# Chunked attention and a gated feed-forward layer: the first round of products in two token halves, and other places for one unit's load, two units' steps and a scaling

## The chip, the cores and the metric

One core of one Trainium2 chip runs the whole kernel. The metric is the device time of one execution in microseconds; 0.1% of it is 0.9 us.

## What is computed

Attention over chunks of 64 tokens (8 sequences, 8 heads, 576 tokens, head size 64), then root-mean-square normalization and a gated feed-forward layer on 4608 tokens with a model width of 512 and an inner width of 1536, all in float32:

```python
scores = scale * q_c @ k_c.T                    # per chunk of 64 tokens and head
attn = exp(scores - max(scores)); attn /= sum(attn) + 1e-9
x = (attn @ v_c) as (4608, 512)
xn = x / sqrt(mean(x * x) + 1e-6) * rms_g
g = xn @ w_gate
out = (g * sigmoid(g) * (xn @ w_val)) @ w_out
```

## The kernel before

**Products.** A float32 operand is split into a high and a low part that TensorE multiplies at its faster float32 rate; a product of two split operands is three matmuls, high by high, high by low and low by high. Tokens go in blocks of 512 (t = 0 to 8). A block's tokens, transposed, stand in four pairs of tiles, `xh[dt]` and `xl[dt]` (dt = 0 to 3, 128 of the 512 model columns each). The inner width goes in 12 slices of 128 (f = 0 to 11); for each, 12 matmuls of 128x512 make `ps_g` and 12 make `ps_v`. ScalarE takes the silu of `ps_g` (`sg`, line 583 or 619), VectorE multiplies it by `ps_v`. The banks of `ps_g` (and in block 0 of `ps_v`) come from a pool of two.

**Units.** Attention goes in units of 256 tokens, two to a block. Units 0 and 1 stand ahead of all products. Their tokens are transposed and split by `x_transpose_unit` (line 546): transposes into one bank for two dts, then for each dt `x_split`, a scaled copy on ScalarE (the high part, line 523) and a subtraction on VectorE (the low part, line 524).

**Block 0 (t = 0).** Units 2 and 3 are computed between its products. The weights come as 64-bit numbers and are converted on the fly, `conv_start`, `conv_join` and `conv_end` (lines 183 to 220), mostly on VectorE. `gated(f, ...)` (line 574) calls `up` twice, then silu, product and split into `gh` and `gl`; `down` (line 624) multiplies the result of the slice before with `w_out`. A unit's tokens are normalized by `norm_unit` (line 490); its inner function `scale` (line 512), called at f = 4 and 9, multiplies them by `ri_u`, which GpSimd makes (line 510). From f = 9 on, `out_sides` (line 649) makes sums of `w_out` on VectorE (lines 659, 667, 672) for later blocks. At f = 11, `x_transpose` (line 536) brings the tokens of units 2 and 3 into `xh` and `xl`. In this part the framework's planner orders each engine's instructions, by program order, by what is ready in its own model of time, and with the instructions under `urgent()` ahead.

**Blocks 1 and 2.** Here each engine's order is the program's own. `gated_pair` (line 595) makes a slice's 24 products, and after each group of 12 one step of a hand-written list runs, 48 steps in all (step 0 to 23 in block 1, 24 to 47 in block 2; where a slice is taken by dt, its two steps stand at its end). The list `at` is filled in the loop over `UNIT_AT` (line 41), then with `sides` and `out_sides`. For each of the units 4 to 9, `UNIT_AT` has the steps of its 11 parts in `unit_steps` (line 1030 on): load of q and k (one buffer for all units), scores and exponentials (`first`), load of the values (a buffer shared with the tokens, two in all), sums and turn (`second`), away to DRAM, back as `eT` (`third`, line 377, one buffer), products with the values and norm (`fourth`, lines 392, 406, 462), scaling (line 417), turn (line 423), away (line 428), back into `x` (line 435). Within a step the units come in order of their number, then the sums of the weights. All these DMAs stand on SP's one queue in program order. At f = 11 of block 1 the tokens of units 4 and 5 replace those in `xh` and `xl` dt by dt (the turn-over); units 6 and 7 come into `x` after that. GpSimd makes the sums of the other weights (`sides`, line 690), in steps `SIDE_AT`, and the small steps of a norm.

The later blocks take two token blocks at a time by another scheme and are not touched.

## Time and profile before

| what | us |
|---|---|
| median of 3 runs | 904.32 (903.79 to 904.64) |
| the profiled execution | 903.54 |
| its span in the profile | 901.8 |
| TensorE busy | 875.2 (97%) |
| VectorE busy | 672.1 (75%) |
| ScalarE busy | 438.1 (49%) |
| GpSimd busy | 171.6 (19%) |

The profile is one execution, 0.78 us under the median; 1.7 us of it lie outside the span. Times in rows are from the span's start. TensorE's column PE is matmuls, PEld its weight loads, which go on beside them; the ends of matmuls are modelled, so a row's duration is longer than the distance to the next one's start, and it is the distance that counts. A row with an idle time in brackets tells what ended the engine's wait. A share of busy time over the whole span says little: the 75% of VectorE is far more in the first block and less later.

### The profile page before, as it was taken

Reading aid. Unit: us, or ns where it says so; the run is one execution under the profiler, and the core shown is the slowest. Engines: PE = TensorE matmul, PEld = TensorE weight load, DVE = VectorE, ACT = ScalarE, POOL = GpSimd, SP = SyncE. Lnnn points to the kernel's source line nnn. Section 1 sums busy time; section 2 is a strip of 40 time slices with the busy share of each in tenths; the row PEclk is TensorE's granted clock in tenths of the full one; section 3 lists DMA queues with packets and bytes.
Section 4 is the critical chain, followed back from the end, with each engine's and each line's share of the span. In section 5 each row is a group of like instructions: output and inputs, shape, how many; then the busy total and the mean of one; then the engine's idle time right before and its main releaser. Section 6 shows DMA issues by size and latency. Waiting matters only on the chain.

```text
span 901.8 us, 17138 instructions
## 1 busy us (share of the span) xinstructions
PE 875.2 (97%) x6792; PEld 715.4 (79%) x6792; DVE 672.1 (75%) x1083; ACT 438.1 (49%) x733; POOL 171.6 (19%) x213
## 2 busy tenths in 40 slices
PE   5799999999999999999999999999999999999998
PEld 4588878877888888888877888888878888888886
DVE  6999996788686887876577988756679974345885
ACT  5997944446353663433355644334536532112452
POOL 0100005395670000112221001122210002111000
PEclk9999999999999999999999999999999999999999
DMA  9698966879879967489877884898689677445623
GB/s 358 267 376 311 312 242 218 268 240 289 252 232 312 293 240 266 162 308 350 259 271 233 302 300 164 303 291 316 238 255 330 256 297 266 152 156 191 217 72 116
DMA packets 96512, 231.82 MB, mean 257 GB/s; under 512 B 7344, under 2 KB 63664, under 8 KB 81072
## 3 DMA queue, kind: packets, MB, share of 16 engines
q1 hardware_dynamic: 95376, 230.19, 73.9%
q8 instruction: 54, 0.88, 0.4%
q10 hardware_dynamic: 1056, 0.52, 0.2%
q14 instruction: 26, 0.21, 0.1%
HBM read 171.97 MB, written 58.72 MB: 256 GB/s over the span
## 4 chain that ended last, share of the span: by engine, by line
PE 74%; DVE 8%; issue 6%; ACT 6%; DMA 4%; POOL 1%; SPq 1%; ACTq 0%; DVEq 0%; POOLq 0%
PE ps_a L794 10%; PE ps_c L794 10%; PE ps_b L794 10%; PE ps_a L975 7%; PE ps_b L975 7%; PE ps_c L975 6%; PE ps_d L794 5%; PE ps_g L606 5%; PE ps_v L606 4%; PE ps_d L975 4%; PE ps_s L269 1%; PE ps_o L392 1%; DMA wr<-wsd 1%; PE acc L629 1%; DVE ab L723 1%
## 5 line engine op out<-in xcount | busy, mean ns | idle before, releaser
L894 ACT CAST gh<-g 128x512 fp32r<-128x512 f32 x140 | 81.7, 620 | 75.5 <-PE ps_b L975 21.3
L895 DVE TENSOR_TENSOR gl<-g,gh 128x512 fp32r<-128x512 f32 x140 | 95.3, 688 | 30.3 <-ACT gh L894 29.3
L794 PE MATMUL ps_c<-xp,wr 128*128 128x512 f32 x432 | 104.7, 391 | 0.0
L794 PE MATMUL ps_b<-xp,wr 128*128 128x512 f32 x432 | 104.4, 391 | 0.0
L794 PE MATMUL ps_a<-xp,wr 128*128 128x512 f32 x432 | 103.7, 390 | 0.4 <-DMA wr<-wsd 0.4
L794 PEld LDWEIGHTS ps_a<-xp,wr 128*128 128x128 f32 x432 | 80.9, 188 | 17.6 <-issue 0.8
L794 PEld LDWEIGHTS ps_c<-xp,wr 128*128 128x128 f32 x432 | 80.7, 188 | 17.1
L794 PEld LDWEIGHTS ps_b<-xp,wr 128*128 128x128 f32 x432 | 80.6, 188 | 16.9
L859 POOL TENSOR_TENSOR g<-c,c 128x512 f32<-128x512 f32 x18 | 23.2, 1291 | 359.1 <-DVE c L855 269.0
L606 PE MATMUL ps_g<-xh,parts 128*128 128x512 f32 x192 | 65.8, 396 | 1.1 <-ACT sg L619 1.1
L606 PE MATMUL ps_v<-xh,parts 128*128 128x512 f32 x192 | 66.2, 398 | 0.0
L975 PE MATMUL ps_a<-gh,wo 128*128 128x512 f32 x176 | 55.9, 389 | 0.0
L794 PE MATMUL ps_d<-xp,wr 128*128 128x512 f32 x216 | 51.9, 389 | 0.0
L975 PE MATMUL ps_c<-gh,wo 128*128 128x512 f32 x160 | 51.1, 392 | 0.2 <-ACT gh L894 0.2
L975 PE MATMUL ps_b<-gh,wo 128*128 128x512 f32 x160 | 50.5, 389 | 0.0
L794 PEld LDWEIGHTS ps_d<-xp,wr 128*128 128x128 f32 x216 | 40.5, 188 | 8.4
L937 DVE TENSOR_TENSOR g<-g 128x512 f32<-128x512 f32 x68 | 46.6, 686 | 0.0
L835 ACT ACTIVATE c<-c 128x512 f32<-128x512 f32 x18 | 11.4, 635 | 68.1 <-DVE c L855 68.0
L606 PEld LDWEIGHTS ps_v<-xh,parts 128*128 128x128 f32 x192 | 36.3, 189 | 10.1 <-issue 2.1
L606 PEld LDWEIGHTS ps_g<-xh,parts 128*128 128x128 f32 x192 | 36.5, 190 | 9.6 <-ACT sg L619 1.6
L844 DVE TENSOR_TENSOR u<-ps_b,p 128x512 f32<-128x512 f32 x36 | 24.0, 685 | 25.2 <-PE ps_b L794 24.0
L695 POOL TENSOR_TENSOR ab<-parts 128x256 f32<-128x256 f32 x48 | 37.3, 810 | 23.5 <-DVE xl L524 23.5
(176 smaller groups left out, 1872.3 us busy)
## 6 DMA issues: line engine op xcount, KB each, us to landing
wr<-wsd SPq DMA_DIRECT2D x63, 1024.0 KB, 8.5
qk<-qk_dram SPq DMA_DIRECT2D x17, 1024.0 KB, 6.9
wo<-wol SPq DMA_DIRECT2D x16, 1024.0 KB, 8.0
raw<-w_up_dram SPq DMA_DIRECT2D x12, 1024.0 KB, 13.0
wo<-wod SPq DMA_DIRECT2D x12, 1024.0 KB, 9.4
vt<-v_dram SPq DMA_DIRECT2D x18, 512.0 KB, 5.8
wsd<-parts SPq DMA_DIRECT2D x18, 512.0 KB, 8.3
wo<-wol SPq DMA_DIRECT2D x16, 512.0 KB, 7.6
```

The costliest lines, as they stand in the source:

```text
L269: nc.tensor.matmul(st["s"][j][c * CH : (c + 1) * CH, pr], st["q"][rows, pr, tok : tok + CH], st["k"][rows, pr, tok : tok + CH], start=True ...
L392: nc.tensor.matmul(st["o"][(2 * c + t) * Q : (2 * c + t + 1) * Q, h * D : (h + 1) * D], eT[rows, c, t, h], vt[rows, c, h], start=True, sto ...
L606: nc.tensor.matmul(ps[k], a, b[dt], start=(dt == 0 and i == 0), stop=(dt == NDT - 1 and i == 2), skip_group_check=True,)
L695: return nc.gpsimd.tensor_tensor(out, one, two, op=op)
L794: nc.tensor.matmul(ps, w[:, a, m, cols], xp[:, b, kt], start=start and kt == 0 and i == 0, stop=stop and kt == 1 and i == 2, skip_group_ch ...
L835: nc.scalar.activation(t, t if src is None else src, AF.Silu)
L844: nc.vector.tensor_tensor(kp["u2"], b["b"], kp["p1"], op=add)
L859: nc.gpsimd.tensor_tensor(g[1][1], kp["c22"], kept[0]["c22"], op=mult)
L894: nc.scalar.copy(gh, src)
L895: nc.vector.tensor_tensor(gl, src, gh.bitcast(F32), op=ALU.subtract)
L937: nc.vector.tensor_tensor(out, one, two, op=ALU.subtract)
L975: nc.tensor.matmul(ps[m][INTO[p]], w[:, m, a], parts[c], start=p in FROM and i == 0 and j == 0, stop=p in LAST and i == NPR - 1 and j == 2 ...
```

## The change

Three edits. First, `gated(0)` calls `up_halves` instead of `up` twice: its products are taken for the first 256 tokens, then for the second, 48 matmuls of 256 columns instead of 24 of 512, with the products of all `xh` ahead of those of `xl`; and `x_transpose_unit` makes the high parts of both dts of a bank before the low parts. Second, each scaling in `scale` is ordered on ScalarE behind the last silu that was written before it. Third, `UNIT_AT` changes for the units 6 and 7 (the third and fourth line), and unit 7's load goes to the head of its step.

```diff
 UNIT_AT = (
     (-1, 0, 3, 2, 3, 5, 8, 10, 10, 11, 13),
     (0, 4, 7, 6, 7, 9, 12, 14, 14, 15, 17),
-    (5, 10, 16, 12, 14, 16, 25, 27, 27, 28, 31),
-    (11, 15, 27, 17, 19, 27, 32, 34, 34, 35, 38),
+    (5, 10, 13, 12, 14, 15, 18, 20, 20, 21, 25),
+    (13, 15, 20, 17, 19, 21, 26, 28, 28, 29, 32),
     (22, 28, 34, 30, 32, 34, 39, 41, 41, 42, 45),
     (29, 34, 40, 36, 38, 40, 45, 46, 46, 48, 51),
 )
...
         def scale():
             for s in range(2):
-                nc.scalar.mul(xu[:, s], xu[:, s], ri[:, s : s + 1])
+                ins = nc.scalar.mul(xu[:, s], xu[:, s], ri[:, s : s + 1])
+                info = mybir.DependencyInfo(mybir.DependencyClass.NoSync, mybir.DependencyReason.DATA)
+                tc.add_manual_dep(ins.ins, silu_last[0].ins.name, info, reason="gates go first")
...
+    def x_split(dt, pt, cols):
+        x_high(dt, pt, cols)
+        x_low(dt, pt, cols)
...
             for s in range(2):
...
-            for i in range(2):
-                x_split(2 * half + i, pt[:, i], cols)
+            for go in (x_high, x_low):
+                for i in range(2):
+                    go(2 * half + i, pt[:, i], cols)
...
+    def up_halves():
+        both = bank(ps_h, "ps_g"), bank(ps_h, "ps_v")
+        for half in range(2):
+            cols = slice(half * UT, (half + 1) * UT)
+            for ps, wh, wl in zip(both, (wgh, wvh), (wgl, wvl)):
+                todo = [(a, xh, dt) for dt in range(NDT) for a in (wh, wl)]
+                todo += [(wh, xl, dt) for dt in range(NDT)]
+                for n, (a, b, dt) in enumerate(todo):
+                    nc.tensor.matmul(
+                        ps[:, cols],
+                        a[0][:, dt * P : (dt + 1) * P],
+                        b[dt][:, cols],
+                        start=n == 0,
+                        stop=n == len(todo) - 1,
+                        skip_group_check=True,
+                    )
+        return both
+
     def gated(f, at, then):
-        pg = up(wgh, wgl, f, "ps_g")
-        pv = up(wvh, wvl, f, "ps_v")
+        if f == 0:
+            pg, pv = up_halves()
+        else:
+            pg = up(wgh, wgl, f, "ps_g")
+            pv = up(wvh, wvl, f, "ps_v")
...
-            nc.scalar.activation(sg, pg, AF.Silu)
+            silu_last[0] = nc.scalar.activation(sg, pg, AF.Silu)
...
-    for n, u in enumerate(range(4, 10)):
-        todo = unit_steps(u, lambda n=n: xx[n >= 4])
+    units = [unit_steps(u, lambda n=n: xx[n >= 4]) for n, u in enumerate(range(4, 10))]
+    do(UNIT_AT[3][0], units[3][0])
+    for n, todo in enumerate(units):
         for k, f in zip(UNIT_AT[n], todo):
-            if k >= 0:
+            if k >= 0 and f is not units[3][0]:
                 do(k, f)
```

## Rows read from the trace of the kernel before

**Rows 1.** The page, part 1: busy time of each engine (its share of the span) and its instructions.

```profile
PE 875.2 (97%) x6792; PEld 715.4 (79%) x6792; DVE 672.1 (75%) x1083; ACT 438.1 (49%) x733; POOL 171.6 (19%) x213
```

**Rows 2.** The waits of TensorE (PE) over the whole span: engine, line and tile, what it waited for: us in total, times, longest.

```profile
PE ps_x L554 <- ACT x L488: 4.4, 2, 3.5
PE ps_v L606 <- issue: 1.9, 1, 1.9
PE ps_s L269 <- ACT ps_o L462: 0.2, 1, 0.2
```

**Rows 3.** Two windows: from:to in us and the length, then busy time of each engine (instructions), the granted TensorE clock, the mean busy share of the DMA engines and GB/s.

```profile
100.00:120.00 20.00, 20.00 (x152) 16.52 (x151) 19.08 (x27) 17.16 (x29) 0.00 (x0) 1.00 0.92 302
200.00:204.00 4.00, 4.00 (x52) 3.32 (x45) 3.10 (x4) 2.70 (x4) 3.84 (x5) 1.00 0.00 0
```

**Rows 4.** The timeline from 26 to 43 us: start, duration (us), engine, line, operation, tiles out<-in, shapes, how many in a row; in brackets the idle time of the engine before it and what ended it.

```profile
27.21 1.22 DVE L220 TENSOR_TENSOR parts<-w,parts 128x1024 fp32r<-128x1024 f32 x1 [0.18 <-ACT parts L214]
33.10 1.11 PE L554 MATMUL ps_x<-ident,x 128*128 128x128 f32 x4 [3.53 <-ACT x L488]
34.42 0.80 PE L565 MATMUL ps_g<-xh,parts 128*128 128x512 f32 x1 [0.20 <-ACT xh L523]
36.74 0.81 ACT L523 ACTIVATE xh<-ps_x,g_col 128x256 fp32r<-128x256 f32 x2
37.22 0.88 DVE L524 SCALAR_TENSOR_TENSOR xl<-ps_x,g_col,xh 128x256 fp32r<-128x256 f32 x2 [0.71 <-ACT xh L523]
40.85 0.60 ACT L583 ACTIVATE sg<-ps_g 128x512 f32<-128x512 f32 x1
41.36 0.39 PE L565 MATMUL ps_v<-xh,parts 128*128 128x512 f32 x1
42.77 0.50 PE L565 MATMUL ps_g<-xh,parts 128*128 128x512 f32 x1
```

**Rows 5.** The chain of waits from 120 to 262 us: start, duration of a piece (us), engine, tile, line, instructions in it. Both pieces are products in a row without a wait.

```profile
126.85 2.72 PE ps_v L565 x12
142.70 0.87 PE ps_x L540 x8
```

**Rows 6.** The timeline from 112 to 128 us, columns as in rows 4.

```profile
121.95 1.34 ACT L514 ACTIVATE x<-x,ri_u 128x512 f32<-128x512 f32 x2 [2.24 <-POOL ri_u L510]
123.19 0.58 ACT L583 ACTIVATE sg<-ps_g 128x512 f32<-128x512 f32 x1
123.83 0.50 PE L565 MATMUL ps_g<-xh,parts 128*128 128x512 f32 x1 [1.57 <-ACT sg L583]
```

**Rows 7.** The timeline around 102 to 105 us and 140 to 142 us, columns as in rows 4; then three groups of VectorE's instructions from 40 to 142 us by line: operation, tiles, shapes, count, busy us, mean ns of one, idle us before them.

```profile
102.14 1.22 DVE L220 TENSOR_TENSOR parts<-w,parts 128x1024 fp32r<-128x1024 f32 x1
104.91 0.39 PE L565 MATMUL ps_g<-xh,parts 128*128 128x512 f32 x1
...
140.41 0.69 DVE L592 TENSOR_TENSOR gl<-sg,gh 128x512 fp32r<-128x512 f32 x1
141.63 0.39 PE L629 MATMUL acc<-parts,gl 128*128 128x512 f32 x1
...
L659 DVE TENSOR_TENSOR w<-parts 128x1024 f32<-128x1024 f32 x2 | 2.4, 1222 | 0.0
L667 DVE TENSOR_TENSOR w<-w 128x256 f32<-128x256 f32 x8 | 3.2, 424 | 0.0
L672 DVE TENSOR_TENSOR parts<-w,parts 128x1024 fp32r<-128x1024 f32 x2 | 2.4, 1222 | 1.1 <-ACT parts L671 1.1
```

**Rows 8.** The timeline, VectorE at 186.70 us and TensorE at 212.76 us, columns as in rows 4.

```profile
186.70 2.44 DVE L723 TENSOR_TENSOR ab<-ab,side 128x512 fp32r<-128x512 f32 x2 [1.21 <-ACT side L722]
...
212.76 0.50 PE L606 MATMUL ps_g<-xh,parts 128*128 128x512 f32 x1 [1.14 <-ACT sg L619]
```

**Rows 9.** One window, columns as in rows 3, and two products that follow each other in it, columns as in rows 4.

```profile
192.00:194.00 2.00, 2.00 (x6) 1.51 (x6) 1.93 (x6) 0.74 (x2) 1.75 (x5) 0.50 0.85 230
...
192.64 0.63 PE L606 MATMUL ps_v<-xh,parts 128*128 128x512 f32 x1
193.07 0.63 PE L606 MATMUL ps_g<-xh,parts 128*128 128x512 f32 x1
```

**Rows 10.** SP's queue, its timeline from 144 to 275 us, columns as in rows 4; then, for the tile eT from 144 to 275 us, the time from issue to landing of its DMAs; then one piece of the chain of waits, columns as in rows 5.

```profile
205.38 0.32 SPq L428 DMA_DIRECT2D away_x<-xu  x1
208.60 2.74 SPq L377 DMA_DIRECT2D eT<-away_e  x4
...
DMA to landing us min/median/max: 2.4/4.5/5.6
...
230.06 1.41 PE ps_o L392 x91
```

**Rows 11.** VectorE around the turn-over of the tokens and at unit 6's norm and turn, columns as in rows 4; then ScalarE's casts of side from 216 to 228 us, columns as the groups of rows 7 with what ended the idle time.

```profile
223.74 2.08 DVE L524 SCALAR_TENSOR_TENSOR xl<-x,g_col,xh 128x512 fp32r<-128x512 f32 x3
...
231.49 1.29 DVE L406 TENSOR_TENSOR xu<-ps_o,rs 128x512 f32<-128x512 f32 x2 [0.65 <-PE ps_o L392]
237.85 1.24 DVE L423 STREAM_TRANSPOSE xu<-xu 128x1024 f32<-128x1024 f32 x1
...
L722 ACT CAST side<-ab 128x512 fp32r<-128x512 f32 x4 | 2.5, 624 | 5.8 <-DMA wsd<-side 3.7 <-DVE rs L354 2.2
```

**Rows 12.** SP's queue, columns as in rows 4: the load of unit 7.

```profile
182.82 0.39 SPq L239 DMA_DIRECT2D qk<-qk_dram  x1
```

More of the change, by code (lines that the diff above doesn't have):

```diff
@@ L522, in x_split, with x_high, x_low @@
             hi, lo = (w.rearrange("p (n c) -> p n c", c=2 * Q) for w in (hi, lo))
+        return g_col[:, dt : dt + 1], hi, lo
+    def x_split(dt, pt, cols):
+        x_high(dt, pt, cols)
+        x_low(dt, pt, cols)
+    def x_high(dt, pt, cols):
+        g, hi, _ = x_parts(dt, pt, cols)
         nc.scalar.mul(hi, pt, g)
+    def x_low(dt, pt, cols):
+        g, hi, lo = x_parts(dt, pt, cols)
         split_last[0] = nc.vector.scalar_tensor_tensor(
```

4 lines of the change are left out of this document (2 added, 2 removed).

## The prediction, made before the changed kernel was run

> **What bounds the kernel now.** I read the page's engine shares first: TensorE is busy 97% of the span [rows 1], so a change gains only where TensorE stands still or works at the lower clock. The list of its waits names the places [rows 2]: 4.4 us before two token transposes, 1.9 us with no releaser, 0.2 us behind a unit's norm; to these come two waits for a gate on ScalarE, 1.57 us near 122 us and 1.14 us near 212 us [rows 6, 8]. The windows [rows 3] then show who else sets the pace: in the first block VectorE is busy 19.08 of 20 us. An early start of TensorE is therefore kept only as far as VectorE's results come earlier too. One fifth of a percent, 1.8 us, is about what a measurement here tells from no change.
>
> **The start: products by 256 tokens.** Today the first product starts at 34.42 us, when the second 256 tokens have been transposed and their first xh is made; the last two dts' xh come at 36.74 us, and the 24 products end at about 41.7 us [rows 4]. The weights are whole at 27.21 + 1.22 = 28.4 us, about when the first 256 tokens are split, and TensorE stands idle 3.5 us before 33.10 us [rows 4]. Twenty-four products of 256 columns go there. At the lower clock 512 columns take 0.43 us [rows 9], so half takes from 0.21 to, say, 0.27 us, 5.1 to 6.5 us in all; begun at 28.4 us they end at 33.5 to 34.9 us, up to 1.8 us past the transposes' place. I take 0.5 us of delay for these. The second half is then bound by its tokens: xh of the last dt at 37.55 + 0.5, its xl at 38.1 + 0.5 = 38.6 us. If the order leaves the 12 products of ps_v behind, they follow at the upper clock. No row has 256 columns there; 512 take 2.72 / 12 = 0.227 us and 128 take 0.87 / 8 = 0.11 us [rows 5]; I take 0.14 us, nearer to the small one by columns: 38.6 + 12 x 0.14 = 40.3 us, against 41.7 us, so 1.4 us. Upper end: no delay and four products left, 38.7 us, a gain of 3.0 us. Lower end: all 48 behind the second transposes at 0.227 us, 10.9 us against the 7.3 us of today, 3.6 us lost; with the first half beside idle time I take 1.4. ScalarE allows it: the first silu ends at 41.45 us and the products of f = 1 start at 42.77 us in the bank that it frees [rows 4], so 1.3 us is kept even if its order stays. Making high parts before low ones costs nothing: ScalarE makes them in pairs already [rows 4].
>
> At the upper clock a 512-column product follows the last by 0.227 us, 0.013 us over 512 / 2.4 GHz [rows 5], although each product has a weight load of its own [rows 1]: the loads are hidden. The Trainium skill ("TensorE: Matmul & The Clock Gate", Part 3, The mechanism) says that a load overlaps running products only where it goes to another row group; the trace differs. By that page's load figure 24 added loads would cost an estimated 24 x 0.107 = 2.6 us.
>
> **The scaling behind the gate.** ScalarE waits 2.24 us for GpSimd's ri_u with two scalings, and the silu of f = 9 stands behind them and ends at 123.77 us; TensorE waits 1.57 us for its bank [rows 6]. After the change the silu goes first. Behind the waiting scalings there then stand a cast and the next gates; the scaled tokens are first needed by the transposes at f = 11, two rounds of products later. Gain 1.57 us; 0 if VectorE holds TensorE back anyway. The other scaling, of f = 4, stands behind its silu already: nothing.
>
> **What VectorE lets through.** At f = 8 the low weights end at 103.36 us and the third product uses them at 104.91 us: 1.5 us to spare [rows 7], so the 1.4 passes. At the block's end gl of f = 11 is made from 140.41 to 141.10 us and used at 141.63 us: 0.5 us to spare. There the two gains, 3.0 us, pass only if VectorE makes it earlier. Among what it does ahead of it are sums of w_out, 2.4 + 3.2 + 2.4 = 8.0 us, that no product of this block uses [rows 7]; the order in this part is the planner's, with gates marked urgent. I take it that the gate moves ahead of the last of them: 3.0 us kept at the end of the block. Ends: 0.5 us and 1.57 + 3.0 = 4.6 us.
>
> **The moved steps of units 6 and 7.** Here the order is written by hand. Unit 6's products and norm go from step 25 to 18, scaling and turning from 27 to 20; unit 7's from 32 to 26 and from 34 to 28. Today TensorE waits until 212.76 us for a silu that stands behind a line of work on VectorE which starts at 186.70 us [rows 8], has unit 5 turned at 205.4 us, when SP can send it away [rows 10], and goes on with exponentials. The stop of 1.92 us at 190.37 us [rows 2] and the clock behind it (granted 0.50, 1.2 GHz, from 192 to 194 us: eight products at 0.43 instead of 0.227 us, 1.6 us [rows 9]) cost nothing of their own: without them TensorE would stand at the same silu sooner. So what counts is how late step 18 and the turn-over of the tokens come.
>
> Step 18 needs eT of unit 6. Its four DMAs are issued from 208.60 to 211.3 us today; with landings of 2.4 to 5.6 us, here near 5, the last is there at 215.7 us, and nothing uses it until 230.06 us [rows 10]. One step up, they stand on SP's queue directly behind away_x at 205.38 us, ahead of two stores: the last is issued at 207.9 us. I take the shortest landing, 2.4 us, since the DMA engines stood still from 200 to 204 us [rows 3]: 210.3 us. TensorE comes to step 18 one group and the wait of 1.14 us before 212.76 us, at 208.9 us, or, without the stop, 3.5 us sooner, and waits. Then ps_o, 1.41 us [rows 10], three groups of 2.72 and the 5.44 us of f = 11, and 1.6 us for the clock, as at 190 us: 226.9 us. The turn-over asks for the same time: its first xl is ready at 224.5 us today, and ahead of it VectorE now has the norm, 1.29 us, and the turn, 1.24 us [rows 11]: 227.0 us. ScalarE's two squares and two scalings, about 0.7 us each by their size (128x512), 2.8 us, I cost at nothing: it waited 5.8 us in that stretch, mostly for saves of side [rows 11]; without that cover they are 2.8 us more. So the second block starts at 226.9 instead of about 224.3 us, 2.6 us later, less the 1.41 us that ps_o costs at 230 us today [rows 10], less the wait of 0.2 us behind unit 7's norm [rows 2]: 1.0 us lost. Ends: nothing (no VectorE or clock price, 226.0 us) and 6.4 us lost (rival B).
>
> The rest is covered. GpSimd's small steps stand behind sums and ahead of none until step 25. Unit 7's load, issued at 182.82 us today [rows 12], goes two steps later on SP, behind the saves, some 7 us; its products come at step 15, two groups of 2.72 us and the landing later: a wait of a microsecond, spent before the one at step 18. The four x DMAs behind it, 0.4 us later, are used at the turn-over. Unit 7's eT now stands behind unit 6's away_x, a step behind its turn; five groups of 2.72 us lie between that and step 26, more than a landing of 5 us and the issue need.
>
> **Sum.** 1.4 + 1.57 - 1.0 = 2.0 us off. The profiled execution took 903.54 us (span 901.8), 0.8 us under the median of 904.32; from it 901.5, and for the median 902.3 us.
>
> **Rivals.** A: VectorE keeps its order, gl of f = 11 stays at 141.1 us and 0.5 us passes: 904.3 - 0.5 + 1.0 = 904.8 us. For it: its share; against: the 8 us of sums. B, slower: eT of unit 6 lands no sooner than today, at 215.7 us. TensorE idles at step 18, drops to 1.2 GHz, and starts the second block at 215.7 + 1.4 + 13.6 + 1.6 = 232.3 us, 8.0 - 1.6 = 6.4 us lost: 904.3 - 3.0 + 6.4 = 907.7 us. It decides from a landing at 210.3 us on, 1 us for each; from 212.3 us the gain is gone. For it: the same four DMAs needed 5 us; against: an empty queue. C: the planner leaves the halves behind the second transposes and the first part does nothing: 904.3 - 1.57 + 1.0 = 903.7 us. D: loads do not hide behind 256 columns, 12 products at 0.227 us, 1.0 us more: 903.3 us. That is what the rule on loads would do; [rows 5] speaks against it. E: the start gives 3.0 us and the moved steps fit into waits: 904.3 - 4.6 = 899.7 us.
>
> **Chances.** The forecast 0.35 (901.0 to 903.4 us, three quarters under the 902.5 us that count as faster), A 0.22, B 0.13, C 0.12, D 0.03, E 0.15. Faster 0.26 + 0.15 + a little of C: 0.43; slower B and a tenth of A: 0.15; the same 0.42. The range from 899.7 to 905.0 us leaves out B and the far side of E.
>
> **What would show it.** Right: products of 256 columns between 28 and 34 us, f = 1 from about 41.4 us; no wait on the silu near 122 us; a wait of TensorE on eT near step 18 that ends with the landing. Wrong: gl of f = 11 still at 141 us (A), that wait over 6 us (B), no products before 33 us (C), 256 columns at 0.2 us at the upper clock (D).

## The result and the profile after

| | us (median, range, runs) | profiled span |
|---|---|---|
| before, same chip | 903.54 (903.10 to 904.64, 6) | 901.8 |
| after | 909.11 (908.33 to 911.30, 6) | 907.2 |

The ratio is 1.0063 [1.005, 1.0076]: slower by 5.6 us, where 902.3 us (899.7 to 905.0) was forecast. The sign was wrong.

Part 1 of the page of after answers to [rows 1], the list of TensorE's waits (us in total, times, longest) to [rows 2]:

```profile
PE 875.9 (97%) x6816; PEld 717.1 (79%) x6816; DVE 671.3 (74%) x1083; ACT 441.6 (49%) x737; POOL 176.1 (19%) x213
```

```profile
...
PE ps_o L392 <- DMA eT<-away_e: 3.0, 1, 3.0
PE ps_g L578 <- DVE parts L220: 2.1, 2, 1.2
PE ps_o L392 <- issue: 1.8, 1, 1.8
...
PE ps_g L578 <- ACT parts L214: 1.6, 2, 1.3
...
PE ps_s L269 <- DMA qk<-qk_dram: 1.0, 2, 0.7
```

The shares hardly moved; the waits did. The 4.4 us ahead of the token transposes are gone (1.5 us ahead of the first products stand there instead), and new are waits on converted weights (L214, L220), on eT and on q and k, and two stops with no releaser. Lines of after lie up to 37 higher: L565 is L578, L583 is L620, L606 is L643, L629 is L666; L598 is the new `up_halves`.

What decides is where the time lies. The ledger cuts TensorE's timeline at four instructions: its first matmul of all (the scores of unit 0, near 5 us), the first with `w_out` (L629, L666), the first of the second block (L606, L643), and the first output product of the later scheme. Each column is the distance between two cuts; the last is the two powers that GpSimd makes for the norms in block 0 (L510). All kernels of the experiments stand in it, one profiled execution each; the later part, where no edit changes an instruction, varies from 601.54 to 604.71 us among them, but for the three kernels with a new tile named root (606.70 to 608.17).

| kernel | to first w_out product | rest of block 0 | blocks 1 and 2 | later | span | powers |
|---|---|---|---|---|---|---|
| before | 43.47 | 96.44 | 154.72 | 602.24 | 901.75 | 1.07, 1.68 |
| after | 40.82 | 100.94 | 156.90 | 603.32 | 907.19 | 1.15, 7.42 |
| start_alone | 41.15 | 102.52 | 155.60 | 602.25 | 906.70 | 1.15, 7.42 |
| units_alone | 43.77 | 96.08 | 157.95 | 602.91 | 905.80 | 1.07, 1.69 |
| scale_alone | 43.66 | 95.83 | 154.85 | 601.54 | 901.03 | 1.07, 1.69 |
| split_alone | 43.96 | 103.77 | 155.45 | 602.30 | 910.60 | 6.89, 3.94 |
| halves_alone | 43.07 | 96.39 | 154.87 | 603.78 | 903.06 | 1.61, 2.81 |
| scale_late | 40.80 | 100.21 | 156.64 | 602.38 | 905.07 | 1.16, 7.42 |
| start_scale_late | 41.59 | 100.19 | 154.85 | 604.71 | 906.39 | 1.16, 7.42 |
| unit6_late | 41.57 | 100.99 | 154.89 | 601.88 | 904.27 | 1.15, 7.42 |
| before_late_sums | 44.50 | 95.97 | 172.06 | 602.08 | 919.61 | 1.07, 1.69 |
| start_late_sums | 40.95 | 99.07 | 170.59 | 601.64 | 917.42 | 1.16, 6.28 |
| start_root | 40.82 | 99.88 | 156.78 | 606.70 | 909.20 | 1.07, 1.07 |
| start_root_late_sums | 40.84 | 98.89 | 170.64 | 608.17 | 923.49 | 1.07, 1.07 |
| before_less_vector | 45.00 | 100.07 | 155.49 | 604.15 | 909.70 | 2.21, 2.20 |
| start_less_vector | 41.21 | 98.59 | 155.49 | 604.36 | 904.68 | 1.60, 1.07 |
| start_root_less_vector | 41.40 | 98.18 | 156.38 | 607.80 | 908.85 | 1.61, 1.07 |
| start_root_in_place | 40.80 | 99.85 | 154.83 | 603.83 | 904.42 | 1.07, 1.07 |
| after_root_unit6 | 40.77 | 99.87 | 156.00 | 603.08 | 904.75 | 1.07, 1.06 |
| before_root_in_place | 44.41 | 96.32 | 155.65 | 602.41 | 903.95 | 1.07, 1.60 |

After less before: -2.65 at the start, +4.50 in the rest of block 0, +2.18 in blocks 1 and 2, +1.08 later, and 0.33 ahead of the first matmul; together +5.44 us, the 5.4 us of the spans. The forecast was 2.0 us off. Of the 7.4 us between the two, 4.8 lie in block 0: 3.0 us were to be kept at its end, and, counted from the first matmul, the second block starts 1.85 us later (141.76 against 139.91). Another 1.2 us lie in the moved steps (1.0 forecast, 2.18 measured), and 1.4 where nothing was forecast.

The start went as meant. Of the timeline of after, TensorE from 28 to 41 us (start, duration, engine, line, operation, tiles, shapes, how many; in brackets idle time and its releaser), which answers to [rows 4]:

```profile
28.32 1.91 PE L598 MATMUL ps_g<-xh,parts 128*128 128x256 f32 x8 [1.52 <-DVE x L482]
...
34.40 0.50 PE L598 MATMUL ps_g<-xh,parts 128*128 128x256 f32 x2 [0.52 <-ACT xh L532]
...
36.52 0.28 PE L598 MATMUL ps_v<-xl,parts 128*128 128x256 f32 x1
36.65 0.28 PE L598 MATMUL ps_g<-xl,parts 128*128 128x256 f32 x1
36.77 0.28 PE L598 MATMUL ps_v<-xl,parts 128*128 128x256 f32 x1
...
40.45 0.50 PE L578 MATMUL ps_g<-xh,parts 128*128 128x512 f32 x1 [0.95 <-ACT sg L620]
```

The products begin at 28.32 us and f = 1 at 40.45 us instead of 42.77 [rows 4]. At the upper clock 256 columns follow each other by 0.12 us (36.52, 36.65, 36.77).

Then the loss. The chain of waits of after, from GpSimd's second power to the end of block 0 (start, duration, what), goes through four engines:

```profile
122.37 7.43 POOL ri_u L510
...
129.82 1.34 ACT x L514 x2
131.16 0.49 ACT sg L620
...
131.67 0.69 DVE sg L624
132.37 1.13 DVE w L203
133.50 0.60 DVE gl L629
134.10 1.15 DVE parts L220
...
135.29 2.56 PE ps_g L578 x10
```

It reads from the top: the power takes 7.4 us, the scaling stands behind it on ScalarE, the silu of f = 10 behind the scaling, VectorE waits for the silu, and the low weights (L220) that TensorE needs at 135.29 us stand behind VectorE's wait. The timeline of after shows the same on each engine, with the wait at 88 us that comes earlier:

```profile
88.44 0.73 PE L578 MATMUL ps_g<-xh,parts 128*128 128x512 f32 x2 [0.89 <-DVE parts L220]
...
129.82 1.34 ACT L514 ACTIVATE x<-x,ri_u 128x512 f32<-128x512 f32 x2 [6.95 <-POOL ri_u L510]
...
131.67 0.69 DVE L624 TENSOR_TENSOR sg<-ps_v,sg 128x512 f32<-128x512 f32 x1 [2.44 <-ACT sg L620]
...
132.62 0.50 PE L578 MATMUL ps_g<-xh,parts 128*128 128x512 f32 x1 [1.32 <-ACT parts L214]
...
135.29 0.73 PE L578 MATMUL ps_g<-xh,parts 128*128 128x512 f32 x2 [1.23 <-DVE parts L220]
```

Block 0 has the same 608 matmuls behind its first `w_out` product in both kernels. Taken from start to start, the stops in after come to 0.44 and 0.45 us at 58 us, 1.05 at 88.4, 1.48 at 132.6 and 1.40 at 135.3, together 4.82; in before there is one, 1.73 us [rows 6]. That is 3.1 of the 4.5 us; the other 1.4 are tenths spread over the block. No instruction of ScalarE or VectorE waits for a DMA from 28 to 145 us in either kernel, so the loads of the weights are not what is late.

The moved steps, the timeline of after on SP's queue and TensorE, a window there (columns as in [rows 3]), and for the tile eT from 200 to 222 us the time from issue to landing of its DMAs, against [rows 8 to 10]:

```profile
206.83 0.32 SPq L428 DMA_DIRECT2D away_x<-xu  x1
207.25 2.20 SPq L377 DMA_DIRECT2D eT<-away_e  x4
...
211.22 0.27 PE L392 MATMUL ps_o<-vt,eT 64*32 64x64 f32 x2 [3.04 <-DMA eT<-away_e]
212.48 1.91 PE L392 MATMUL ps_o<-vt,eT 64*32 64x64 f32 x126 [0.99 <-DVE ab L760]
```

```profile
212.90:216.20 3.30, 3.30 (x104) 2.74 (x97) 1.16 (x2) 2.75 (x5) 3.06 (x5) 0.50 1.08 381
```

```profile
DMA to landing us min/median/max: 3.3/3.4/3.5
```

The four eT land between 210.50 and 212.34 us. The second stop is put down to VectorE, but it ends 0.14 us behind the last landing: it is eT again. Then the granted clock is 0.50 (1.2 GHz) for 3.3 us.

### The profile page after: what moved, and what is told of

Read it like the earlier page. It is cut to its first block, busy times and chain, and to the rows that moved or that the text cites. A ratio compares the mean times of both kernels' runs of the same rounds, so it can differ in the third digit from the quotient of the medians.

```text
span 907.2 us, 17199 instructions
## 1 busy us (share of the span) xinstructions
PE 875.9 (97%) x6816; PEld 717.1 (79%) x6816; DVE 671.3 (74%) x1083; ACT 441.6 (49%) x737; POOL 176.1 (19%) x213
## 4 chain that ended last, share of the span: by engine, by line
PE 77%; ACT 6%; issue 6%; DVE 5%; DMA 3%; POOL 2%; SPq 0%; ACTq 0%; POOLq 0%; DVEq 0%
PE ps_c L831 10%; PE ps_b L831 10%; PE ps_a L831 10%; PE ps_a L1012 7%; PE ps_b L1012 7%; PE ps_c L1012 7%; PE ps_v L643 6%; PE ps_g L643 6%; PE ps_d L831 5%; PE ps_d L1012 4%; PE ps_o L392 2%; PE ps_s L269 2%; ACT raw L190 1%; POOL ri_u L510 1%; DMA wr<-wsd 1%
## 5 line engine op out<-in xcount | busy, mean ns | idle before, releaser
L643 PE MATMUL ps_v<-xh,parts 128*128 128x512 f32 x192 | 66.3, 399 | 1.6 <-issue 1.6
L643 PE MATMUL ps_g<-xh,parts 128*128 128x512 f32 x192 | 64.9, 391 | 0.0
L643 PEld LDWEIGHTS ps_v<-xh,parts 128*128 128x128 f32 x192 | 36.4, 190 | 10.0 <-issue 2.0
L732 POOL TENSOR_TENSOR ab<-ab 128x256 f32<-128x256 f32 x48 | 41.8, 875 | 2.8
L643 PEld LDWEIGHTS ps_g<-xh,parts 128*128 128x128 f32 x192 | 36.0, 188 | 7.7
```

The costliest lines, as they stand in the source:

```text
L643: nc.tensor.matmul(ps[k], a, b[dt], start=(dt == 0 and i == 0), stop=(dt == NDT - 1 and i == 2), skip_group_check=True,)
L732: return nc.gpsimd.tensor_tensor(out, one, two, op=op)
```

## The experiments

Ratios are to before on the same chip, with the 95% interval. Each expectation names the theories that stood at that time. On the changed start the order of instructions is the same on every engine with and without the scaling's edit, so there it makes no difference which kernels carry it.

### The parts alone

**units_alone**: before with the new `UNIT_AT` of units 6 and 7 and unit 7's load ahead.

```diff
-    (5, 10, 16, 12, 14, 16, 25, 27, 27, 28, 31),
-    (11, 15, 27, 17, 19, 27, 32, 34, 34, 35, 38),
+    (5, 10, 13, 12, 14, 15, 18, 20, 20, 21, 25),
+    (13, 15, 20, 17, 19, 21, 26, 28, 28, 29, 32),
```

> The kernel before with only the moved steps of units 6 and 7 (and unit 7's load issued ahead). Theory A, the sum of differences read between the two traces: the wait for unit 6's turned weights, the lower clock behind it and the steps around 240 us cost 5.2 us, the stop at 190 us stays since TensorE's instructions ahead of it are those of before: 908 to 909.5. Rival B, the steps cost only what the wait itself shows (4.4 us less the 1.1 us wait of before that it takes the place of), and the other part of the 5.2 us is a stop of instruction fetch that falls elsewhere in this stream: 906.5 to 907.5. Rival C, the prediction's price of the steps (1.0 us): 904.5.

**start_alone**: `up_halves` and the high parts first, nothing else.

```diff
+        if f == 0:
+            pg, pv = up_halves()
...
-                x_split(2 * half + i, pt[:, i], cols)
+            for go in (x_high, x_low):
+                for i in range(2):
+                    go(2 * half + i, pt[:, i], cols)
```

> The kernel before with the first round by 256 tokens and high parts ahead of low ones, nothing else; the order of instructions on each engine up to 180 us is that of the changed kernel. Theory A: 2.3 to 2.7 us gained by 42 us, 4.5 us given back by the end of the first block, the stop of 1.9 us and the low clock behind it near 190 us gone (2.9 us), a stop near 489 us new (1.5 us): 902.4 without the last, 903.9 with it. Rival B, the loss of the first block in the profiled execution was a rare one (a power on GpSimd that took 7.42 us in place of 1.68): 898 to 900. Rival C, the prediction's terms (3.0 us kept): 900.5.

**scale_alone**: before with only the scalings behind the silu.

```diff
...
+                tc.add_manual_dep(ins.ins, silu_last[0].ins.name, info, reason="gates go first")
...
```

> The kernel before with only the scaling of tokens tied behind the gate's activation; it swaps two instructions on ScalarE near 122 us and no other order on any engine. The prediction's bounds: the wait of 1.57 us at 123.83 goes (902.0), or VectorE's weights come no sooner and nothing changes (903.5). Theory A holds neither against the other: it has no row for it, since the changed kernel has the same order with and without this tie. Rival: the second block starts later, as the scaling is now late for the token products: 904 to 905.

**split_alone**: only the high parts ahead of the low ones (the second hunk of start_alone).

```diff
...
+            for go in (x_high, x_low):
...
```

> The kernel before with only the order of the first block's token splits changed (both high parts, then both low parts), the products still by 512 tokens. Theory A: the gain at the start is the halves' and absent here; the orders of the conversions on VectorE and ScalarE change too, so block 0 moves by its own waits: 903 to 905. If the high parts ahead of low ones is what gains, f=1 starts 1 us or more sooner than 42.8 us and the time is 902 or less. If the changed conversion order is what costs the 4.5 us, they show here without the gain of the start: 906 or more.

Measured: units_alone 1.0023 [1.0009, 1.0037], start_alone 1.0051 [1.0035, 1.0067], scale_alone 0.999 [0.9981, 1.0], split_alone 1.0073 [1.0059, 1.0086]. The three come to 0.23 + 0.51 - 0.10 = 0.64% against 0.63% of the whole, but that they fit so well is chance: on the changed start the scaling's edit changes no order, so the sum to compare is 0.23 + 0.51 = 0.74%, which agrees within the intervals. So the start, which was to bring 1.4 us, costs most, and the order of the splits, which I had at nothing, costs more alone than the start as a whole. Start_alone costs more than any of its theories had, units_alone less than A and B and more than C, and of split_alone's cases the third came true, that the order of the conversions costs. In the ledger split_alone loses 7.3 us in block 0, with powers of 6.89 and 3.94 us.

Units_alone has the same kinds of stops as after, for q and k and for eT, and one more with no releaser:

```profile
198.74 1.16 PE L269 MATMUL ps_s<-qk 64*64 64x64 f32 x64 [1.69 <-DMA qk<-qk_dram]
...
210.71 1.41 PE L392 MATMUL ps_o<-vt,eT 64*32 64x64 f32 x120 [1.32 <-DMA eT<-away_e]
213.24 0.43 PE L392 MATMUL ps_o<-vt,eT 64*32 64x64 f32 x6 [1.13 <-issue]
```

Scale_alone does near 122 us what was forecast, but most of it doesn't reach the end of block 0. Its timeline:

```profile
119.82 0.57 ACT L620 ACTIVATE sg<-ps_g 128x512 f32<-128x512 f32 x1
122.15 1.34 ACT L514 ACTIVATE x<-x,ri_u 128x512 f32<-128x512 f32 x2 [1.76 <-POOL ri_u L510]
...
140.61 0.69 DVE L629 TENSOR_TENSOR gl<-sg,gh 128x512 fp32r<-128x512 f32 x1
...
140.63 0.73 PE L666 MATMUL acc<-parts,gh 128*128 128x512 f32 x2 [0.23 <-ACT gh L625]
...
211.85 0.50 PE L643 MATMUL ps_g<-xh,parts 128*128 128x512 f32 x1 [2.50 <-ACT sg L656]
```

The silu of f = 9 stands ahead of the scaling and TensorE's stop near 122 us is gone, but block 0 is only 0.6 us shorter. The gl of f = 11 is made until 141.30 us, no sooner than in before (141.10 [rows 7]); TensorE, which comes there sooner, now waits, and first uses gl at 141.35 us. At the silu of the next block it waits 2.50 us instead of 1.14 [rows 8], but blocks 1 and 2 as a whole are only 0.13 us longer: the lower clock, which in before comes behind the stop near 190 us [rows 9], is not there from 192 to 194 us (granted 1.00) and comes behind this wait instead, where gate 10 takes 7.20 us (5.58 in before).

**halves_alone**: only `up_halves`, the splits in the old order.

```diff
+        if f == 0:
+            pg, pv = up_halves()
```

> The kernel before with only the first round by 256 tokens, the splits in their old order. Theory D: the time follows how long GpSimd's power for the scaling takes in whatever order the conversions get: with 1.7 us, 901 to 902 (the start's gain kept); with 4 us or more, 906 or more. Rival G: it is the smaller products' own price or VectorE's total, and block 0 ends late with a short power too.

1.001 [1.0, 1.0019], between the two cases of the expectation, with a second power of 2.81 us. It gains 0.4 us at the start, and nothing is lost in block 0. Its timeline says why the gain is small: the high parts of the second half are late behind low ones (the idle time ahead of the products at 37.28 us).

```profile
37.28 0.98 PE L598 MATMUL ps_g<-xh,parts 128*128 128x256 f32 x6 [2.04 <-ACT xh L532]
```

So the start's gain needs both edits, and the cost comes with the order of the splits.

### The scaling's wait in the changed kernel

**scale_late** (on after) and **start_scale_late** (on start_alone): the second scaling is written one slice later.

```diff
-            elif f in (4, 9):
+            elif f in (4, 10):
                 scale()
```

> The changed kernel with the second scaling of tokens called one gate later (behind the activation of gate 10 in place of gate 9); only ScalarE's order changes, the scaling now stands behind that activation. Theory D: what gives back the start's gain is ScalarE standing 6.95 us at the scaling for GpSimd's power (7.42 us here, 1.68 us before) with gate 10's activation and a conversion behind it, so TensorE's waits at 132.62 and 135.29 us (1.48 and 1.40 us) go: 906 against 909 of the changed kernel. Rival E: VectorE's own work is what is late there, and the waits move to the next weights: 908.5 to 909.5. Rival F: the scaling is then late for the next block's token products: 910 or more.

> The kernel before with the whole first-block part of the change (256 tokens at a time, high ahead of low, scaling tied to a gate), the scaling called one gate later, and units 6 and 7 as before. Theory D: of the 4.6 us that the start alone cost, the two waits (2.9 us) and the lower clock behind them (1.9 us) go; 0.998 to 1.000 of before (903 to 904.5). Rival E: 908, as the start alone. If the start's gain of 2.3 us comes through in full besides, 901 to 902.

1.0046 [1.0029, 1.0062] and 1.0036 [1.0026, 1.0046]. The silu of f = 10 is now free, and the stop near 132 us shrinks to 0.20 us idle, but both times stay above theory D's: the scalings still wait for the power, a cast of weights stands behind the first of them, and L220 behind that. The timeline of scale_late:

```profile
129.64 0.73 ACT L514 ACTIVATE x<-x,ri_u 128x512 f32<-128x512 f32 x1 [3.29 <-POOL ri_u L510]
130.27 1.03 ACT L214 CAST parts<-w 128x1024 fp32r<-128x1024 f32 x1
...
134.34 0.73 PE L578 MATMUL ps_g<-xh,parts 128*128 128x512 f32 x2 [1.58 <-DVE parts L220]
```

In block 0 that is worth 0.7 us against after and 2.3 us against start_alone, in which the granted clock also was 0.50 (1.2 GHz) from 135.9 to 139.2 us, behind these stops. Neither of the two places tried for the scaling is a good one while the power takes 7.4 us.

### The steps of unit 6

**unit6_late**: after, with unit 6's steps from the return of eT on three later.

```diff
-    (5, 10, 13, 12, 14, 15, 18, 20, 20, 21, 25),
+    (5, 10, 13, 12, 14, 15, 21, 23, 23, 24, 28),
```

> The changed kernel with unit 6's values and what follows them 3 steps later (step 21 in place of 18), so that its turned weights (landing until 212.34 us) have landed. Theory A: TensorE's waits of 3.2 and 1.2 us and the lower clock behind them go, and pair 10 starts at the gate activation's end (214.2 in place of 218.1 us): 2.4 to 4 us less than the changed kernel, 905 to 906.7. Rival H: GpSimd's sums, which start with the block, set the pace to about 235 us whatever TensorE does in between, and the step later only moves the wait: 908.5 to 909.5.

1.004 [1.0026, 1.0055]: 0.23%, some 2.1 us, less than after, a little under theory A's 2.4 to 4 us. Blocks 1 and 2 take 154.89 us, 2.0 less than in after and as before (154.72). Its timeline shows the products with the values without a wait, and a longer stop at the silu ahead of them:

```profile
214.73 0.60 PE L643 MATMUL ps_g<-xh,parts 128*128 128x512 f32 x1 [2.79 <-ACT sg L656]
...
222.01 1.48 PE L392 MATMUL ps_o<-vt,eT 64*32 64x64 f32 x128
```

So most of the loss there is put down to unit 6's early step. How much is not sharp: with the old steps, and the sums of `w_out` in block 0, this column runs from 154.72 to 156.78 us (start_root), and with both remedies (after_root_unit6, below) it is 156.00. The stop at the silu stands in before too, with 1.14 us [rows 8].

### Is VectorE's amount of work the bound?

**before_late_sums** and **start_late_sums**: the sums of `w_out` that block 0 makes are left to block 1, on before and on the changed start (with the scaling's order, old units).

```diff
-SUM_AT = 0, 0, 7, 12, 26, 32
+SUM_AT = 0, 3, 7, 12, 26, 32
-EARLY_SUMS = 2
+EARLY_SUMS = 0
```

> The kernel before with the two early sums of w_out (8.0 us of VectorE's work at the end of the first block) moved to steps 0 and 3 of the next block. Theory V: VectorE's work, 130 to 131 us from TensorE's first instruction to the next block in every run so far, plus its idle time sets the end of the first block. Freed of 8.0 us of it, the block is TensorE's, which stood idle 1.57 us there: the next block starts 1.2 to 1.6 us sooner (139.9 us after the first instruction now). The sums then stand beside GpSimd's in the next block, which may cost up to 8 us: 902 to 906 in all. Rival: VectorE is not it, the wait for the gate's activation stays and the next block starts where it did.

> The same two sums moved in the kernel with the whole first-block part of the change and the units' steps of before. Theory V: with VectorE no longer the bound, the start's 2.3 to 2.6 us come through: the next block starts 2 us or more ahead of the run above, 5 to 6 us ahead of the start alone (143.7 us after the first instruction), and the time is 1.5 to 2.5 us under the run above. Theory D (GpSimd's power alone): the waits at the end of the block stay, since ScalarE still stands behind the power: 142 us or more. Rival G (the smaller products' own price): no gain over the run above.

1.0187 [1.0173, 1.02] and 1.0187 [1.017, 1.0204]. The sums are ruinous in block 1 (172.06 and 170.59 us instead of 154.72), beside GpSimd's. What counts here is when the second block starts, from the first matmul of all: 139.91 us in before, 140.47 without the sums; 141.76 in after, 140.02 without them. VectorE worked 130 us to there in before and 124 and 123 us in the kernels without sums, and its idle time rose from 9 to 17 us. In before, then, the amount of VectorE's work doesn't hold the end of the block: with 7 us less of it the block ends no sooner. But in before_late_sums TensorE still stands 1.10 us at 124.51 us, for the silu behind the scaling, so this is no test of rival A, for which a gain has to reach the end of the block; scale_alone is. In the changed kernel the sums do count. Without them the second block starts 1.7 us sooner than in after, at before's place, and the stops near 132 and 135 us shrink from 2.9 to 1.0 us, though the second power still takes 6.28 us. That the power alone makes these stops, with 142 us or more in the expectation, falls; the start's gain doesn't come through either.

**before_less_vector**, **start_less_vector**: the clamp, shift and sign of the first three pairs of converted `w_out` (2.6 us a pair) are left out; those weights have other values.

```diff
+            if pairs[n][0] == "up" or pairs[n][1] > 4:
+                nc.vector.tensor_scalar(w, w, HIGH_LEAST, HIGH_MOST, op0=ALU.max, op1=ALU.min)
...
```

> The kernel before without three of VectorE's steps (clamp, shift, sign) in the conversion of the first three pairs of w_out: 2.6 us of VectorE's work each, spread over the first block; the weights made of them are others. Theory V (VectorE's work, piece by piece, sets when TensorE's weights are there): TensorE is dense here up to 123.83 us and can gain only that wait: the next block 0 to 1.6 us sooner than 139.9 us after the first instruction, the sixth down product (f=5) at 87.8 us after it as before. Rival W (ScalarE's order sets it): the same, so this run is the measure for the next one.

> The same three steps left out for the same pairs in the kernel with the first-block part and the units' steps of before. Theory V: the wait for weights at 88 us goes and the start's gain is still there behind it: the sixth down product at 86 us or less after the first instruction (88.5 with the start alone), the next block at 137.5 to 140 (143.7), and the time 1 to 2.3 us under the run before it. Rival W: VectorE has time to spare and TensorE still waits near 58 and 88 us for what ScalarE makes: 88 or more, and no gain over the run before it.

1.0069 [1.0055, 1.0082] and 1.0017 [1.0008, 1.0026]. The pair can't be used as I meant it: before_less_vector became slower, with another order by the planner, in which VectorE stands idle 21.0 us instead of 9.4 up to the second block. The planner's order is another in start_less_vector too, so what it shows isn't shown to come from the amount of work alone. Its sixth round of `w_out` starts 85.55 us behind the first matmul, against 87.81 in before, 88.12 in after: here, with less for VectorE to do early, the start's gain is kept to there. The same window in three kernels:

```profile
59.80:88.30 28.50, 28.50 (x244) 23.32 (x243) 27.61 (x37) 24.11 (x32) 1.07 (x1) 1.00 0.91 323
```

```profile
59.80:88.30 28.50, 27.71 (x236) 22.36 (x235) 28.29 (x37) 26.15 (x33) 1.15 (x1) 1.00 0.84 302
```

```profile
59.80:88.30 28.50, 28.50 (x243) 23.29 (x242) 26.77 (x35) 24.19 (x32) 1.60 (x1) 1.00 0.98 349
```

In before (the first) VectorE is busy 27.61 of 28.50 us, in after (the second) 28.29, and TensorE stops; in start_less_vector (the third) it is 26.77, and TensorE does not. Then it loses the lead at other waits, 1.49 us at 94.94 (a silu) and 1.73 us at 105.17 (an exponential).

### The power

**start_root**: the changed start; VectorE copies the power's result, and ScalarE reads the copy. That puts a wait for GpSimd on VectorE itself.

```diff
+        root = small.tile([P, 2], F32, name="root")
+        with urgent():
+            nc.vector.tensor_scalar(root, ri, 1.0, None, op0=ALU.mult)
+        ri = root
```

> The whole first-block part with the units' steps of before, and behind GpSimd's power a copy of its 256 results on VectorE, so that VectorE stands still until the power is done. Theory of the port: the power takes 7.42 us because VectorE's instructions follow one another without a gap; with VectorE made to wait it takes 0.55 to 1.5 us, ScalarE's stop of 6.95 us goes, and the next block starts 2 to 4 us sooner than with the start alone (143.7 us after the first instruction): 904.5 to 906.5 against 908.6. Rival: the power is long for a reason of GpSimd's own; then VectorE stands idle with it, 7 us, and the time is 912 or more.

**start_root_late_sums** and **start_root_less_vector**: that with the edits above.

```diff
+EARLY_SUMS = 0            # start_root_late_sums
...
+            if pairs[n][0] == "up" or pairs[n][1] > 4:      # start_root_less_vector
...
```

> Both edits together. Theory V with the port: the next block starts 139 us or less after the first instruction, since neither VectorE's total nor its waits are left, and the time is that of the second run or up to 1 us less. If GpSimd's power is short there already, no difference.

> The run before it, with GpSimd's power copied on VectorE at once, so that it is short. Theory V with the port: if the power is still long in the run before it, the next block starts 1 to 3 us sooner than there; if it is short there, 0.5 to 1 us later, which is what VectorE's stop costs.

1.0071 [1.0058, 1.0085], 1.0225 [1.021, 1.0239], 1.0071 [1.0059, 1.0084]. In start_root both powers now take 1.07 us, because VectorE stops for them, as its timeline shows (against 7.42 in after):

```profile
122.92 1.07 POOL L510 TENSOR_TENSOR ri_u<-ss_u,mhalf 128x2 f32<-128x2 f32 x1 [42.25 <-DVE ss_u L508]
...
124.02 0.17 DVE L513 TENSOR_SCALAR root<-ri_u 128x2 f32<-128x2 f32 x1 [0.59 <-POOL ri_u L510]
```

Block 0 drops from 102.52 us in start_alone to 99.88, with start_alone's order of instructions but for the two copies and three moved ones: the long power did cost time there. But the whole became no faster: the last column of the ledger before the span is 606.70 instead of 602.25. That loss lies in a part that no edit touches. By form, from 500 to 560 us (count, busy us, mean ns), the same products in start_root and then in start_root_in_place:

```profile
L1016 PE MATMUL ps_b<-gh,wo 128*128 128x512 f32 x48 | 15.4, 394 | 0.0
```

```profile
L1015 PE MATMUL ps_b<-gh,wo 128*128 128x512 f32 x48 | 15.1, 389 | 0.0
```

**start_root_in_place**, **after_root_unit6** and **before_root_in_place**: the copy goes into `ss`, with no new tile; on the changed start, on after with unit 6's later steps, and on before with the scaling's order.

```diff
+        with urgent():
+            nc.vector.tensor_scalar(ss, ri, 1.0, None, op0=ALU.mult)
+        ri = ss
```

> The whole first-block part with the units' steps of before; the copy of the power's results on VectorE is written over the mean squares, so no tile is added. If the tile's place made the pitch of the down products 231 to 232 ns, it is 227 again, and the time is what the parts give: the next block 140.7 us after the first instruction (3 us sooner than with the start alone), the rest as with the start alone: 904.5 to 906. If the pitch stays at 231, it is not the tile: 910.

> The changed kernel with both remedies: the power's results copied at once on VectorE (no tile added), and unit 6's values 3 steps later. Theories A and port together: the two named mechanisms hold what the change lost, so the time comes to before's within 2 us (903.5 to 905.5) against 909 of the changed kernel. Rival: one wait only takes the other's place in the block that GpSimd paces, and less than half of the 5 us comes back: 906.5 or more.

> The kernel before with the scaling tied behind the gate and the power's results copied at once on VectorE (no tile added). The power takes 1.07 in place of 1.68 us and ScalarE's order is free of it: 0.998 to 1.000 of before, the wait of 1.57 us at 123.83 us gone. Rival: VectorE's stop of 0.9 us costs as much as it gives and the planner's other order with it: 1.000 to 1.003.

1.0028 [1.0018, 1.0037], 1.0026 [1.0013, 1.004], 1.0003 [0.9994, 1.0013]. Without the new tile the products are as fast as ever, block 0 keeps the gain (99.85 us), and the changed start costs 0.28% instead of 0.51%. With both remedies the whole change costs 0.26% instead of 0.63%: 3.3 of the 5.6 us go with them, the other 2.3 us do not, and before's time within 2 us, which the expectation stood for, isn't quite reached. With the sums gone as well (start_root_late_sums) the second block starts 139.73 us behind the first matmul, 1.0 sooner than in start_root, but not at 139 or less. On before the gain that was expected (0.998 to 1.000) doesn't come: the second power takes 1.60 us there with the copy and not 1.07, the rival's range (1.000 to 1.003) holds, and the copy brings nothing over scale_alone. No version beats before by more than the 0.2% that can be told; scale_alone is the nearest.

## Why the prediction was wrong, point by point

**The start: right in kind, larger than forecast.** First products at 28.32 us (forecast 28.4), f = 1 at 40.45 (forecast 41.4), 2.65 us won to the first `w_out` product where 1.4 was taken and 3.0 was the upper end. 256 columns take 0.12 us at the upper clock (0.14 taken). Rivals C and D fall. The Trainium skill ("TensorE: Matmul & The Clock Gate", Part 3, The mechanism) has two rules on this: by its list a load overlaps running products only in another row group, by its text also when it goes to the background weight buffer. The first, which the prediction took up, isn't borne out: 48 loads of 128 columns stand behind products of 256 columns, and the products still follow by 0.12 us; the second would fit.

**High parts before low ones at nothing: wrong.** "ScalarE makes them in pairs already" looked at ScalarE's cost alone. The planner makes another order of the block behind it, and the run with this edit alone costs 0.73%.

**"What VectorE lets through: 3.0 us kept": the step that failed.** I read 1.5 us of slack at 104.91 us and 0.5 us at the end of the block [rows 7], took the 1.4 us to pass at the first, and the planner to move the gate ahead at the second. Nothing passed: the second block starts 1.85 us later than in before. Of the 2.65 us of lead, 0.86 are left at the fifth round of `w_out` (78.65 us behind the first matmul, 79.51 in before) and none at the sixth (88.12, 87.81): VectorE, which is busy 28.29 of 28.50 us ahead of it, had the low weights of that slice ready only at 88.39 us. The slack of one product late in the block isn't the slack of the products before it. Rival A named the right engine. What it says of the block's end, that the gl of f = 11 stays and 0.5 us passes, is what scale_alone shows, where 0.6 us passed; in the changed kernel the lead was gone before it got there, and A's gain of 0.5 us had the wrong sign.

**The scaling, +1.57 us: wrong.** Alone it gave 0.6 us in block 0 and 0.1% in all (0.9981 to 1.0, no more than can be told): the stop of 1.57 us went, and the gl of f = 11 came no sooner. I had asked what waits behind the scaling for two rounds, "a cast and the next gates", and cost it at nothing, with a wait for GpSimd of 2.24 us in mind [rows 6]. In the changed kernel this wait became 6.95 us, and the silu of f = 10 and the weights stood behind it: 132.62 and 135.29 us. That GpSimd's small step could grow was nowhere in the sum, nor in a rival. Of the 4.8 us missed in block 0 it is a part: after_root_unit6 has 1.1 us less there than after, start_root_in_place 2.7 us less than start_alone, which also had the lower clock from 135.9 us on. It isn't the only cause of these stops: without the sums, start_late_sums has 1.9 us less than after with a power of 6.28 us.

**The moved steps, -1.0 us: right in kind, mis-sized.** The wait at step 18 ends with the landing, and the clock falls behind it, as told; so is the microsecond for unit 7's q and k (1.0 us in two stops, and 1.69 in units_alone). The four DMAs landed in 3.3 to 3.5 us (2.4 taken), the last at 212.34 us, 2.0 us behind the forecast of 210.3; the block itself had begun 2.2 us later than in before. The cost was 2.18 us in after, 3.23 alone. But the time of the landing isn't what made the term too small: in units_alone, whose block 1 begins with before's, the last one came at 210.57 us, 0.3 behind the forecast. What was not in the term is the stop of 1.13 us with no releaser behind it, and a lower clock that lasts longer: granted 0.50 from 213 to 219 us, so that the twelve products from 213.60 us take 5.29 us instead of 2.72, 2.6 us more where 1.6 were taken. Rival B's point ("from 212.3 us the gain is gone") is met by its number only, since the gain was gone in block 0; its full price of 6.4 us didn't come.

**The stop near 190 us at nothing: right, with one thing missed.** It is absent from after, and nothing was gained by it. From the second block's start to the first product of its gate 10 it takes 67.97 us in before with the stop, and 68.02 in start_alone: the block goes at the pace of work on other engines. But without it TensorE waits 4.09 us for the silu there (1.14 in before), and the lower clock comes behind this wait: gate 10 takes 7.18 us in start_alone, with a granted clock of 0.63 in its first 3.3 us, and 5.58 in before.

**What remains open.** First, the 0.26% with both remedies. In block 0 with a short power, 99.85 us against 96.44, the stops left are 0.46 and 0.45 us at 58 us, 1.81 at 89 and 1.20 at 134, all but one behind converted weights; why the planner's order has them, and whether another order would keep the lead, wasn't tried. No kernel starts the second block sooner than 139.46 us behind the first matmul (halves_alone; 139.91 in before), whichever wait was taken away; what holds it there isn't shown. The scaling's edit without the sums wasn't run on before, which would have tested whether the gl of f = 11 can come sooner. Then the 1.08 us of the later part of after: a stop of 1.81 us with no releaser stands at 489.42 us, but 1.08 us is also less than this part varies by among kernels in which it is the same.

## What to carry to other kernels

Time won at the head of a stage is kept only if the engine that feeds the stage has room at every product on the way, not at the one whose slack was read; where it is busy 97% of the stretch, as VectorE was here, look first for what stops when it becomes 99%. When an edit makes one engine run without a gap, look at the small steps of the engines that stand beside it, above all a GpSimd step between two VectorE steps: its time is not a constant. And a step moved earlier needs its input earlier by as much: count from the issue of its DMA, with the usual landing and not with the shortest, and add what the lower clock costs behind the wait.

## What the runs showed of the hardware

**A step on GpSimd waits out VectorE's run.** The power on 128x2 elements took from 1.06 to 7.42 us. The timelines of before, after and split_alone:

```profile
120.23 1.68 POOL L510 TENSOR_TENSOR ri_u<-ss_u,mhalf 128x2 f32<-128x2 f32 x1 [42.56 <-DVE ss_u L508]
```

```profile
122.20 0.69 DVE L199 TENSOR_SCALAR w<-w 128x1024 int32<-128x1024 int32 x1
...
122.37 7.42 POOL L510 TENSOR_TENSOR ri_u<-ss_u,mhalf 128x2 f32<-128x2 f32 x1 [41.43 <-DVE ss_u L508]
...
128.01 1.23 DVE L696 TENSOR_TENSOR w<-parts 128x1024 f32<-128x1024 f32 x1
```

```profile
77.86 6.89 POOL L510 TENSOR_TENSOR ri_u<-ss_u,mhalf 128x2 f32<-128x2 f32 x1 [45.80 <-DVE ss_u L508]
123.82 3.94 POOL L510 TENSOR_TENSOR ri_u<-ss_u,mhalf 128x2 f32<-128x2 f32 x1 [39.07 <-DVE ss_u L508]
```

In after VectorE runs without a gap from 122.20 to 129.24 us (128.01 + 1.23), and the power ends at 129.79, 0.55 us later; in split_alone the runs end at 84.19 and 127.21 us and the powers at 84.75 and 127.76, 0.56 and 0.55 later. In start_late_sums the run is one instruction shorter and ends at 128.18 us; the power takes 6.28 us and ends at 128.73, again 0.55 later. Where VectorE was made to stop, it took 1.07 us in start_root and 1.60 in before_root_in_place, ending 0.56 and 0.55 us behind the VectorE instruction that ran. The Trainium skill ("SBUF — State Buffer", section "Who interferes with whom") says that VectorE and GpSimd share a pair of ports, and that, when VectorE is in a two-port mode, whoever issues first holds the pair for its whole instruction while the other is blocked. The trace agrees that GpSimd's step waits for VectorE, but here it is passed over for eight VectorE instructions in a row and not for one; that the ports are the reason no run shows. Why it got in after 1.68 us in before, and after 1.15 us at 79.79 us in after, amid runs just as dense, stays open.

**A tile of 8 bytes went with slower products that don't use it.** With `root` added to its pool, the products whose weights are gh and gl follow each other by 231 to 232 ns instead of 227 (mean duration 394 instead of 389 ns), about 4 us in the later part (606.70 against 603.83 with the copy in place). It was in all three kernels with the tile and in none without; that it is the place of the tiles behind it wasn't tested apart.

**Stops with no releaser.** They come and go with the order of TensorE's stream. In after:

```profile
240.66 0.50 PE L643 MATMUL ps_v<-xh,parts 128*128 128x512 f32 x1 [1.64 <-issue]
...
489.42 0.33 PE L392 MATMUL ps_o<-vt,eT 64*32 64x64 f32 x12 [1.81 <-issue]
```

Each ends 2.3 to 2.5 us after a 16 KB fetch of instructions begins (238.31 and 486.94 us in after; 187.94 in before, for its stop at 190.37). There are 54 such fetches in a kernel, and most are followed by no stop; that the fetch is the cause was not tested.
